# Attention products of 64 rows for two heads in place of 32 rows for four, with warming steps spread over the first batch, V on one queue and a new order of work

## The chip, the core and the metric

The kernel runs on one core of one Trainium2 chip. The metric is the device time of one execution in microseconds (us); lower is better. Five kinds of queues work side by side and each takes its instructions strictly in the order in which the kernel lists them: TensorE (PE, matrix products; its weight loads are shown apart as PEld), VectorE (DVE), ScalarE (ACT), GpSimd (POOL) and SyncE (SP, which only issues transfers). An instruction that waits holds up all that is listed behind it on its engine.

## The reference

For 8 batches, 8 heads, 576 positions and a head size of 64, the kernel computes causal attention in a window of 64 positions, puts the heads side by side (512 features), and feeds the result to a gated network with a spatial product. Cut to what matters:

```python
scores = scale * q @ k.T                        # per batch and head, 576 x 576
attn   = softmax(where(0 <= pos_q - pos_k < 64, scores, -1e9))
x      = (attn @ v), heads side by side          # 576 x 512 per batch
h      = relu(x @ w_in); u, v = h[..., :512], h[..., 512:]
v_n    = (v - mean(v)) / sqrt(var(v) + 1e-6)     # over the 512 features
v_s    = w_spatial @ v_n + b_spatial             # over the 576 positions
out    = (u * v_s) @ w_out
```

## The kernel before, in words

All work is cut into named steps. A step's name begins with its kind and holds its batch, and often its group `g` (heads 0 to 3, or 4 to 7), its pair of heads `u` within the group, or its block of 128 rows. Dependencies and buffers are declared with each step (`add(...)`), but the order on every engine, the engine itself and the buffer numbers come from one long hand-over string, `ORDER` (line 18 on): each word is `step:engine:buffers`. `DQ` is the transfer queue of SP. The costs that stand beside the steps (such as `("PE", 0.52)`) served whoever made the order; they do not act on the chip.

The steps, in the order in which one batch goes through them:

- `ldk`, `ldq` (line 382), `ldv` (line 404): loads of K, Q and V of a group. V comes in five pieces a group, `ldv{b}_{g}{c}`. For the very first group the five pieces are issued from ACT's queue (`dq = nc.scalar`), all others from SP's.
- `ck`, `cq`: casts of K and Q to 16 bits; `tk`, `tq`: their transposes on DVE (line 389). `cv`, `sl`, `su`, `s4`: the cast of V and the copies that make a second V, shifted by half a block. These casts and copies run on ACT (line 280), or on DVE or POOL (line 282), as the order says.
- `S` (line 457): scores of a group, in tiles of 32 rows by 64 columns, into a pair of PSUM tiles. `S{b}_r` (line 528) is the remainder, the last 64 positions of both groups.
- `E` (line 464): the exponential on ACT; `M` (line 467): the window mask, a minimum on DVE.
- `Z` (line 476): the sums of the softmax, products with a block of ones. Four heads are done side by side: each has 32 of the 128 output rows, and one PSUM bank holds all four. `Z{b}_r` (line 550) does it for the remainder.
- `N`, `n` (lines 508 and 510): the inverse of the sums, by a logarithm and an exponential on ACT, on 128 x 512 values for a group, 128 x 128 for the remainder.
- `P` (line 492): the products with V. A product gives 32 rows: every second feature of one head (`vhalf`), so that four heads lie side by side in a bank and the even and odd features in two banks (`f` = 0, 1). A group has 64 such products of 64 columns. `P{b}_r` (line 564) is the remainder.
- `X` (lines 501 and 572): the product with the inverse sums on DVE. Since features of a block are every second one of the heads, the rows of `w_in` are loaded with a step of two (line 308).
- `V{b}_j` (line 635), `V{b}_4` (lines 648 and 651), `U` (lines 690 and 695): products with `w_in`; `Vr` (line 615), `Ur` (line 703): evictions with relu on ACT; `Vb`, `Va` (lines 617 and 619): statistics on DVE; `L1`, `L2`: the inverse deviation on ACT; `A` (line 674): the normalization on DVE.
- `G` (lines 720 and 726): the spatial product; `Ge` (line 734): times u, on DVE; `O` (line 745): the product with `w_out`; `Oe` (line 598): eviction on ACT; `st`: store.

Besides there are the loads, casts and transposes of the weights (`ldwin`, `cwin`, `ldwsp`, `cwsp`, `W`, `We`, `ldwo`, `cwo`). `S` writes to two PSUM tiles of their own; `Z`, `P`, `V`, `U`, `G`, `O` and `W` share four banks, and a step on PE waits until its bank was read.

Ahead of all steps, 16 products of zeros (line 221) keep PE at work while the first loads are on their way.

Of the kernel before, what the change touches and what calls it, by code (L numbers as in the profile page):

```python
# [23 lines left out]
ldwin010:DQ:7 cv0_11:POOL ldwin011:DQ N0_0:ACT:0 s40_1:DVE S0_r:PE:0:1 sl0_11:DVE sl0_01:POOL ldk1_0:DQ:0
M0_10:DVE P0_0:PE:6:5 E0_r0:ACT:0 n0_0:ACT M0_11:DVE cwin100:POOL su0_10:POOL ldq1_0:DQ:1 E0_r1:ACT
su0_11:ACT M0_r:DVE ldk1_1:DQ:2 cwin101:ACT X0_00:DVE:0 Z0_r:PE:4 P0_r:PE:7 ldq1_1:DQ:3 N0_r:ACT:1
cwin111:POOL Z0_1:PE:6 X0_01:DVE n0_r:ACT ldwsp2:DQ:4 X0_r:DVE:0 N0_1:ACT:2 P0_1:PE:4:5 cwin110:DVE
n0_1:ACT ldwsp1:DQ:5 V0_4:PE:7 cwin001:ACT X0_10:DVE:1 X0_11:DVE cwin011:POOL cwin000:DVE V0_2:PE:6
Vr0_4:ACT:0 ldb:DQ:6 cwin010:ACT Vb0_4:DVE:0 ck1_0:POOL:0 ldwsp4:DQ:7 U0_4:PE:4 U0_3:PE:5 tk1_0:DVE:4
ldwsp0:DQ:0 Ur0_4:ACT:0 ldv1_00:DQ:2 cq1_0:POOL:1 Vr0_2:ACT:1 V0_1:PE:7 Va0_4:DVE Vb0_2:DVE:1 V0_0:PE:4  # L30
tq1_0:DVE:5 Vr0_1:ACT:2 ldwsp3:DQ:1 ck1_1:POOL:2 U0_0:PE:6 Vr0_0:ACT:3 Vb0_1:DVE:2 Ur0_3:ACT:1 S1_0:PE:0:1
tk1_1:DVE:0 ldwo10:DQ:2 cq1_1:POOL:3 V0_3:PE:7 E1_01:ACT:0 ldv1_01:DQ Va0_2:DVE cwsp2:POOL tq1_1:DVE:1
U0_1:PE:4 E1_00:ACT:1 ldv1_02:DQ cb:POOL Vb0_0:DVE:3 ldv1_03:DQ cwsp1:POOL Ur0_0:ACT:2 S1_1:PE:1:0
ldv1_04:DQ Vr0_3:ACT:4 M1_01:DVE ldq2_0:DQ:3 U0_2:PE:5 Ur0_1:ACT:3 M1_00:DVE cwsp4:POOL cwsp0:POOL
ldk2_0:DQ:4 E1_10:ACT:2 Vb0_3:DVE:4 ldv1_10:DQ:3 cwsp3:POOL Ur0_2:ACT:4 Va0_1:DVE Va0_3:DVE M1_10:DVE
W0:PE:6 E1_11:ACT:3 ldv1_11:DQ W2:PE:7 Va0_0:DVE W4:PE:4 ldv1_12:DQ We0:DVE cv1_00:POOL:2
W1:PE:5 L10:ACT:0 S1_r:PE:1:0 ldv1_13:DQ M1_11:DVE We1:ACT W3:PE:6 ldv1_14:DQ We2:DVE
cv1_01:POOL L20:ACT We4:ACT Z1_0:PE:5 sl1_00:DVE:2 Z1_1:PE:7 E1_r0:ACT:1 A0_2:DVE:0 N1_0:ACT:3
s41_0:DVE su1_00:POOL A0_1:DVE:1 n1_0:ACT A0_4:DVE sl1_01:POOL A0_0:DVE:2 su1_01:POOL N1_1:ACT:0
We3:DVE ldv2_10:DQ:0 P1_0:PE:4:5 E1_r1:ACT A0_3:DVE:3 cq2_0:ACT:0 M1_r:DVE ldq2_1:DQ:6 G0_0:PE:7  # L40
X1_00:DVE:2 ck2_0:POOL:1 ldv3_10:DQ:1 cwo10:ACT tq2_0:DVE:2 ldwo00:DQ:5 Z1_r:PE:6 n1_1:ACT G0_4:PE:4
ldk2_1:DQ:7 cv1_10:POOL:3 N1_r:ACT:1 ldwo11:DQ X1_01:DVE sl1_10:ACT:3 G0_3:PE:6 ldwo01:DQ Ge0_4:DVE:0
cv1_11:POOL tk2_0:DVE:3 ldq3_1:DQ:0 G0_2:PE:5 sl1_11:ACT su1_11:POOL ldv2_00:DQ:2 n1_r:ACT s41_1:POOL
su1_10:ACT Ge0_3:DVE:1 S2_0:PE:1:0 Ge0_2:DVE:2 P1_1:PE:4:6 ldk4_0:DQ:1 cq2_1:POOL:2 E2_00:ACT:0 Ge0_0:DVE:3
P1_r:PE:5 ldq3_0:DQ:3 X1_10:DVE:3 G0_1:PE:7 E2_01:ACT:1 ldk3_0:DQ:4 X1_11:DVE cwo00:ACT M2_01:DVE
V1_1:PE:4 Ge0_1:DVE:4 ldv2_01:DQ ck2_1:POOL:3 V1_0:PE:6 X1_r:DVE:1 tq2_1:DVE:0 ldv2_02:DQ V1_2:PE:7
Vr1_0:ACT:5 ldv3_00:DQ:3 Vr1_1:ACT:6 M2_00:DVE U1_2:PE:5 cwo11:ACT Vb1_1:DVE:5 Vr1_2:ACT:7 V1_3:PE:6
tk2_1:DVE:1 cwo01:ACT ldv2_03:DQ cq3_1:POOL:0 Z2_0:PE:4 Vr1_3:ACT:1 V1_4:PE:7 Vb1_0:DVE:0 N2_0:ACT:2
ldv2_11:DQ Vb1_2:DVE:1 Ur1_2:ACT:5 S2_1:PE:1:0 Oe0_4:ACT:0 Vb1_3:DVE:2 ck4_0:POOL:1 U1_3:PE:6 Vr1_4:ACT:2
Va1_1:DVE n2_0:ACT Vb1_4:DVE:4 U1_0:PE:4 E2_10:ACT:2 tk4_0:DVE:4 cq3_0:POOL:2 O0_2:PE:5 E2_11:ACT:3  # L50
Va1_2:DVE ldv2_12:DQ Va1_3:DVE O0_0:PE:7 Va1_0:DVE Va1_4:DVE M2_10:DVE Oe0_2:ACT:0 ldv2_13:DQ
M2_11:DVE ck3_0:POOL:3 U1_1:PE:5 Oe0_0:ACT:1 ldv2_04:DQ ldv2_14:DQ L11:ACT:1 O0_3:PE:7 L21:ACT
ldv3_01:DQ Ur1_1:ACT:0 A1_4:DVE Ur1_3:ACT:1 A1_3:DVE:4 ldv3_02:DQ S2_r:PE:1:0 A1_2:DVE:5 cv2_00:POOL:0
Z2_1:PE:5 E2_r0:ACT:0 ldv3_03:DQ tq3_1:DVE:5 U1_4:PE:6 Ur1_0:ACT:4 ldq4_0:DQ:6 N2_1:ACT:3 O0_1:PE:4
ldk3_1:DQ:7 A1_0:DVE:6 sl2_00:ACT:0 A1_1:DVE:7 cv2_10:POOL:1 tq3_0:DVE:0 G1_1:PE:5 Oe0_3:ACT su2_00:POOL
Oe0_1:ACT tk3_0:DVE:1 s42_0:ACT G1_0:PE:7 E2_r1:ACT ldv4_00:DQ:2 sl2_10:POOL:1 Ur1_4:ACT:2 Ge1_1:DVE:5
ldq4_1:DQ:2 P2_0:PE:4:6 s42_1:ACT su2_10:POOL ldk6_0:DQ:5 Ge1_0:DVE:6 n2_1:ACT S3_0:PE:1:0 ldv5_10:DQ:0
X2_00:DVE:0 cv3_00:POOL:2 P2_1:PE:5:7 ldq5_1:DQ:0 E3_00:ACT:0 ldv3_04:DQ X2_01:DVE G1_2:PE:4 st0_0:DQ
E3_01:ACT:1 X2_10:DVE:1 st0_1:DQ ck3_1:POOL:1 G1_3:PE:6 X2_11:DVE cq4_0:ACT:0 Ge1_2:DVE:7 V2_1:PE:5
Ge1_3:DVE:8 M2_r:DVE V2_2:PE:7 M3_00:DVE cq4_1:POOL:2 V2_3:PE:4 tk3_1:DVE:2 Vr2_2:ACT:0 Vr2_1:ACT:3  # L60
V2_0:PE:6 Vr2_3:ACT:4 M3_01:DVE S3_1:PE:1:0 tq4_1:DVE:3 Vr2_0:ACT:2 P2_r:PE:7 sl3_00:ACT:2 Z3_0:PE:5
Z2_r:PE:4 Vb2_2:DVE:3 O1_0:PE:6 N3_0:ACT:0 Vb2_3:DVE:5 N2_r:ACT:1 G1_4:PE:5 n2_r:ACT Vb2_0:DVE:1
n3_0:ACT O1_2:PE:4 E3_11:ACT:2 Va2_2:DVE Ge1_4:DVE:9 X2_r:DVE:0 O1_3:PE:5 Vb2_1:DVE:2 E3_10:ACT:3
M3_11:DVE O1_1:PE:7 Oe1_2:ACT:1 Va2_0:DVE Va2_1:DVE Va2_3:DVE Oe1_0:ACT:0 M3_10:DVE S3_r:PE:0:1
V2_4:PE:4 E3_r0:ACT:1 tq4_0:DVE:0 ck6_0:POOL:3 s43_0:POOL su3_00:POOL ldv4_10:DQ:3 ldv3_11:DQ cq5_1:POOL:1
st0_4:DQ ldv3_12:DQ ldv3_13:DQ ldk4_1:DQ:1 ldk5_1:DQ:3 ldv3_14:DQ Oe1_3:ACT U2_2:PE:6 E3_r1:ACT
Vr2_4:ACT:1 tq5_1:DVE:1 Oe1_4:ACT:0 S4_0:PE:0:1 cv3_10:POOL:3 Ur2_2:ACT:3 st1_4:DQ Vb2_4:DVE:0 P3_0:PE:5:4
Oe1_1:ACT ldq5_0:DQ:4 Z3_1:PE:6 Va2_4:DVE ldv4_11:DQ X3_00:DVE:2 U2_1:PE:7 L12:ACT:0 ldv4_12:DQ
L22:ACT N3_1:ACT:2 X3_01:DVE U2_0:PE:5 st1_0:DQ ck4_1:ACT:2 A2_2:DVE:0 ldv4_13:DQ A2_4:DVE
U2_3:PE:6 A2_3:DVE:1 Ur2_1:ACT:0 A2_1:DVE:2 E4_00:ACT:0 A2_0:DVE:3 U2_4:PE:4 M3_r:DVE G2_1:PE:7  # L70
# [743 lines left out]
```

## Time and profile before

| what | value |
|---|---|
| time, median of 3 runs | 208.84 us (207.15 to 210.27) |
| profiled execution: span from first to last instruction | 206.8 us (the page prints no other time of it) |
| busy: PE, DVE, ACT, POOL | 183.2, 165.0, 142.4, 88.5 us |
| mean granted clock of TensorE | 0.956 |
| first scores of batches 0, 1, 2, 3 | 9.67, 30.04, 45.75, 69.77 us |
| first scores of batches 4, 5, 6, 7 | 84.41, 109.78, 133.48, 154.74 us |
| last product of PE ends | 202.4 us |
| instructions | 7979 |

A profile holds one execution. Busy time of an engine is the time in which it had at least one instruction under way; the granted clock is the share of full speed that TensorE was allowed. A row of the groups gives the line, engine and operation, the tiles written and read with their shapes, then the busy time in us, the mean duration in ns, and the idle time of the engine just before such instructions with what ended it.

### The profile page before, as it was taken

To read this page: it belongs to the slowest core of one execution; us is meant where nothing else is said; L and a number is where in the kernel's file an instruction comes from. 1 tells how busy PE (TensorE), PEld (TensorE's weight loads), DVE (VectorE), ACT (ScalarE), POOL (GpSimd) and SP (SyncE) were. 2 spreads that over 40 slices of the span, in tenths; PEclk is the share of its full clock that TensorE was granted. 3 is DMA by queue.
4 is the path that set the end of the run, shared out by engine and by line. 5 is a ranking of instruction groups with operands and counts; after the bars stand their busy time and mean duration, and the time that the engine had idled before them with its cause. 6 is when DMAs were issued, how large, how long until landed. Compare 5 with 4: busy or idle time off the path is not lost.

```text
span 206.8 us, 7979 instructions
## 1 busy us (share of the span) xinstructions
PE 183.2 (89%) x3465; PEld 94.4 (46%) x3465; DVE 165.0 (80%) x297; ACT 142.4 (69%) x263; POOL 88.5 (43%) x101
## 2 busy tenths in 40 slices
PE   7326899599995999899997899999999999999991
...
DVE  4469899999889799999998689987878768646520
...
PEclk9955699999998899999999999999999999999998
...
GB/s 214 340 211 303 408 310 309 257 267 386 341 182 320 283 284 213 204 236 262 331 263 92 231 324 182 146 331 73 3 3 255 2 3 231 3 2 0 231 81 149
DMA packets 50197, 42.74 MB, mean 207 GB/s; under 512 B 39345, under 2 KB 39345, under 8 KB 50162
## 3 DMA queue, kind: packets, MB, share of 16 engines
...
q10 hardware_dynamic: 2384, 0.59, 1.3%
...
HBM read 32.79 MB, written 9.44 MB: 204 GB/s over the span
## 4 chain that ended last, share of the span: by engine, by line
PE 67%; DVE 17%; ACT 5%; DMA 4%; issue 3%; POOL 1%; SPq 0%; POOLq 0%; DVEq 0%
PE bank L720 16%; PE bank L745 12%; PE bank L635 11%; PE bank L690 10%; PE bank L492 4%; PE bank L648 4%; DVE e L467 4%; DMA nk<-in_k_dram 4%; DVE vn L674 3%; PE pair L457 3%; DVE qT L389 2%; PE bank L726 2%; PE bank L695 2%; DVE hs L282 2%; ACT vs L615 2%
## 5 line engine op out<-in xcount | busy, mean ns | idle before, releaser
L464 ACT ACTIVATE e<-pair 128x1024 f16<-128x1024 f32 x32 | 31.5, 1022 | 20.0 <-PE pair L457 12.5
L720 PE MATMUL bank<-wspT,vn 128*128 128x512 f16 (+1 forms) x160 | 39.8, 392 | 4.5 <-DVE vn L674 3.2
L615 ACT ACTIVATE vs<-bank 128x512 f16<-128x512 f32 (+1 forms) x40 | 23.1, 594 | 16.7 <-PE bank L635 12.9
L734 DVE TENSOR_TENSOR g<-bank,ru 128x512 f16<-128x512 f32 (+1 forms) x40 | 24.6, 629 | 11.8 <-PE bank L720 8.9
L690 PE MATMUL bank<-x,win 128*128 128x512 f16 x128 | 31.5, 379 | 0.1
L635 PE MATMUL bank<-win,x 128*128 128x512 f16 x128 | 30.9, 379 | 0.0
L745 PE MATMUL bank<-wout,g 128*128 128x512 f16 x128 | 30.7, 379 | 0.2 <-ACT ru L703 0.2
L617 DVE BATCH_NORM_STATS2 st<-vs 128x6 f32<-128x512 f16 (+1 forms) x40 | 26.2, 670 | 4.5 <-ACT vs L615 4.2
L703 ACT ACTIVATE ru<-bank 128x512 f32<-128x512 f32 (+1 forms) x40 | 21.8, 556 | 9.1 <-PE bank L695 5.5
L282 POOL CAST hk<-nk 128x1152 f16<-128x1152 f32 x14 | 16.9, 1204 | 25.0 <-DMA nk<-in_k_dram 22.1
L467 DVE TENSOR_TENSOR e<-e,mask 128x1024 f16<-128x1024 f16 x32 | 27.1, 867 | 0.3 <-ACT e L464 0.3
L282 POOL COPY hs<-hv 64x1024 f16<-64x1024 f16 (+3 forms) x29 | 26.1, 902 | 1.4
L282 POOL CAST hv<-nv 128x1024 f16<-128x1024 f32 (+1 forms) x18 | 18.0, 1008 | 19.1 <-DMA nv<-in_v_dram 19.0
L720 PEld LDWEIGHTS <-vn 128*128 128x128 f16 (+1 forms) x160 | 15.0, 100 | 23.4 <-DVE vn L674 4.4
L598 ACT COPY ob<-bank 128x512 f32<-128x512 f32 (+1 forms) x40 | 23.0, 586 | 3.4 <-PE bank L745 2.3
L501 DVE TENSOR_TENSOR x<-bank,lz 128x512 f16<-128x512 f32 x32 | 20.9, 678 | 3.7 <-ACT lz L510 2.4
L389 DVE STREAM_TRANSPOSE kT<-hk 128x576 f32<-128x576 f32 x16 | 19.7, 1239 | 3.7 <-ACT hk L280 2.9
L389 DVE STREAM_TRANSPOSE qT<-hq 128x576 f32<-128x576 f32 x16 | 19.7, 1239 | 1.8 <-POOL hq L282 1.6
L674 DVE TENSOR_SCALAR vn<-vs,mv,ln 128x512 f16<-128x512 f16 (+1 forms) x40 | 18.8, 524 | 2.7 <-ACT ln L664 2.6
L457 PE MATMUL pair<-qT,kT 32*64 32x128 f16 (+2 forms) x1024 | 12.9, 231 | 7.8 <-DVE qT L389 7.5
L745 PEld LDWEIGHTS <-g 128*128 128x128 f16 x128 | 12.1, 98 | 14.7 <-issue 1.0
L635 PEld LDWEIGHTS <-x 128*128 128x128 f16 x128 | 12.0, 98 | 14.5 <-issue 0.6
...
## 6 DMA issues: line engine op xcount, KB each, us to landing
...
```

The source lines that it names most:

```text
L282: ENG[e].tensor_copy(o, i)
L389: d = add(f"t{name}{b}_{g}", ("DVE", 1.09), key, lambda e: nc.vector.transpose(qt.t[:, :].rearrange("p (i j) -> p j i", j=18), h.t[:, :].b ...
L464: ex = add(f"E{b}_{g}{u}", ("ACT", 0.91), key, lambda e, u=u: nc.scalar.activation(e2[u].t[:, :, :], sc[u].t[:, :, :], AF.Exp, bias=0.0, s ...
L467: mins.append(add(f"M{b}_{g}{u}", ("DVE", 0.65), key, lambda e, u=u: nc.vector.tensor_tensor(e2[u].t[:, :, :], e2[u].t[:, :, :], mask[:, : ...
L615: rl = add(f"Vr{b}_{j}", ("ACT", 0.49), key, lambda e: nc.scalar.activation(vs.t[0:jn, :], m.t[0:jn, :], AF.Relu), deps=[pv], acq=[vs], us ...
L617: s1 = add(f"Vb{b}_{j}", ("DVE", 0.6), key + 0.02, lambda e: nc.vector.bn_stats(st6.t[0:jn, 0:6], vs.t[0:jn, :]), deps=[rl], acq=[st6], us ...
L635: nc.tensor.matmul(m.t[:, :], xr(b, r)[:, 128 * j:128 * j + 128], w_in_sb[r][:, 512:1024], start=(r == 0), stop=(r == 3))
L674: ENG[e].tensor_scalar(o[0:jn, :], VS[j].t[0:jn, :], mv_t[b % NSB][0:jn, j, 0:1], ln.t[0:jn, 5 + j:6 + j], ALU.subtract, ALU.mult)
L690: nc.tensor.matmul(m.t[:, :], w_in_sb[r][:, 128 * i:128 * i + 128], xr(b, r), start=(r == 0), stop=(r == 3))
L720: nc.tensor.matmul(m.t[:, :], w[0:kn, 128 * i:128 * i + 128], wspT[kk][0:kn, 0:512], start=(kk == 0), stop=(kk == 4))
L734: lambda e, m=m, g=g, ru=ru, n=n: nc.vector.tensor_tensor(g.t[:, 0:n], m.t[:, 0:n], ru.t[:, 0:n], ALU.mult),
L745: nc.tensor.matmul(m.t[:, :], G[r][0].t[:, 128 * j:128 * j + 128], w_out_sb[r][:, :], start=(r == 0), stop=(r == 3))
```

## The change

In `Z`, `P` and `X` a step now serves a pair of heads, not four. Each product with V gives all 64 features of one head, so that two heads fill the 128 rows of a bank; a group has two steps of `Z` (`Z{b}_{g}{u}`) and two of `P`, each with a bank of its own, where it had one of each with one and two banks. `N` and `n` run once for every pair, so twice a group, on 128 x 512 values; for the remainder on 128 x 256 values. `X` multiplies each pair's products with the pair's own inverse. There are six `lz` buffers for four. The features of a block are now contiguous, and so are the rows of `w_in` that are loaded.

The 16 products of zeros ahead of the steps become 25 steps `D0` to `D24` of two products each, which the order places among PE's work up to the middle of batch 0. The first group's V is issued from SP's queue like the others. The order is written anew as a whole, on all engines: steps stand elsewhere, many casts and copies change their engine, and buffers have other numbers. Counted over the whole order:

| steps | before | after |
|---|---|---|
| `Z` and `P` of groups, on PE | 16 and 16 | 32 and 32 |
| `N` and `n` of groups, on ACT | 16 and 16 | 32 and 32 |
| casts and copies of K, Q, V, weights on POOL | 90 | 64 |
| the same on ACT (`ck`, `cq`, `cv`, `sl`, `su`, `s4`) | 2, 4, 2, 5, 2, 6 | 6, 4, 2, 9, 3, 10 |
| the same on DVE (`ck`, `cq`, `cv`, `sl`, `su`, `s4`) | 0, 0, 0, 2, 2, 2 | 1, 1, 5, 4, 7, 1 |

The diff, cut to its core:

```diff
 ORDER = """
-ldk0_0:DQ:0 ldq0_0:DQ:1 ldk0_1:DQ:2 ldq0_1:DQ:3 ldv0_00:DQ:0 ldv0_01:DQ ldv0_02:DQ ldv0_03:DQ ldv0_04:DQ
-ck0_0:ACT:0 tk0_0:DVE:0 ldv0_10:DQ:1 cq0_0:ACT:1 tq0_0:DVE:1 ldv0_11:DQ ck0_1:POOL:2 S0_0:PE:0:1 tk0_1:DVE:2
-ldv0_12:DQ cq0_1:POOL:3 E0_00:ACT:0 ldv0_13:DQ E0_01:ACT:1 ldv0_14:DQ tq0_1:DVE:3 cv0_00:POOL:0 ldwin100:DQ:4
-sl0_00:POOL:0 M0_00:DVE ldwin101:DQ cv0_01:ACT S0_1:PE:0:1 ldwin110:DQ:5 M0_01:DVE s40_0:POOL ldwin111:DQ
...
+ldq0_0:DQ:0 ldk0_0:DQ:1 D14:PE:0 ldk0_1:DQ:2 ldq0_1:DQ:3 D12:PE:1 ldv0_00:DQ:0 ldq1_0:DQ:4 D23:PE:2
+ldk1_0:DQ:5 ldv0_10:DQ:1 D15:PE:3 cq0_0:POOL:0 ldv0_11:DQ D22:PE:0 D6:PE:1 tq0_0:DVE:0 D0:PE:2
+ck0_0:ACT:1 ldv0_01:DQ D16:PE:3 tk0_0:DVE:1 ck0_1:ACT:2 ldv0_02:DQ S0_0:PE:0:1 tk0_1:DVE:2 D21:PE:0
+E0_00:ACT:0 ldv0_12:DQ D7:PE:1 D11:PE:2 cq0_1:DVE:3 E0_01:ACT:1 ldv0_03:DQ D24:PE:3 tq0_1:DVE:3
+M0_01:DVE cq1_0:ACT:0 ldwin100:DQ:6 S0_1:PE:0:1 M0_00:DVE D5:PE:0 E0_10:ACT:2 tq1_0:DVE:4 D17:PE:1
+D2:PE:2 ldv0_04:DQ E0_11:ACT:3 D4:PE:3 ck1_0:DVE:1 ldv0_13:DQ D1:PE:0 S0_r:PE:0:1 M0_10:DVE
+ldv0_14:DQ Z0_00:PE:1 E0_r0:ACT:0 cv0_10:DVE:0 Z0_10:PE:2 E0_r1:ACT M0_11:DVE ldwin110:DQ:7
+Z0_01:PE:3 N0_10:ACT:0 D10:PE:0 sl0_10:DVE:0 cv0_00:DVE:1 N0_01:ACT:1 ldb:DQ:0 M0_r:DVE N0_00:ACT:2
+sl0_00:DVE:1 Z0_r:PE:2 su0_00:DVE ldwin111:DQ Z0_11:PE:0 N0_r:ACT:3 D9:PE:3 n0_00:ACT cv0_01:DVE
+ldwin101:DQ D8:PE:1 su0_01:DVE sl0_01:POOL n0_10:ACT su0_10:DVE D13:PE:2 ldwin000:DQ:1 n0_01:ACT
...
-    for i in range(16):
-        nc.tensor.matmul(bank(4 + i % 2), scratch[:, 0:128], scratch[:, :], start=True, stop=True)
-    ones = cpool.tile([128, 32], f16, name="ones")
+    ones = cpool.tile([128, 64], f16, name="ones")
...
-                                 st.t[:, 512 * f:512 * f + 512], moe_w_in[256 * g + f:256 * g + 256:2, cs]),
+                                 st.t[:, 512 * f:512 * f + 512], moe_w_in[256 * g + 128 * f:256 * g + 128 * f + 128, cs]),
...
-        dq = nc.scalar if (b, g) == (0, 0) else nc.sync
...
-        zb = buf("bank", f"z{b}_{g}")
-                for hh in range(4):
-                    nc.tensor.matmul(zb.t[32 * hh:32 * hh + 32, :], ones[:, :],
-                                     e2[hh // 2].t[:, hh % 2, :], start=True, stop=True)
...
-        ob = [buf("bank", f"o{b}_{g}{f}") for f in (0, 1)]
-                        for hh in range(4):
-                            nc.tensor.matmul(ob[f].t[32 * hh:32 * hh + 32, 64 * c:64 * c + 64],
-                                             vhalf(vv, c // 2, hh, f),
-                                             e2[hh // 2].t[:, hh % 2, 64 * c:64 * c + 64],
+        for u in (0, 1):
+            zb, ob = buf("bank", f"z{b}_{g}{u}"), buf("bank", f"o{b}_{g}{u}")
+            lz = buf("lz", f"lz{b}_{g}{u}")
+                    for w in (0, 1):
+                        nc.tensor.matmul(zb.t[64 * w:64 * w + 64, :], ones[:, :], e2[u].t[:, w, :],
+                                         start=True, stop=True)
...
+                    for c in range(8):
+                        vv = hv.t if c % 2 == 1 or c == 0 else hs.t
+                        for w in (0, 1):
+                            nc.tensor.matmul(ob.t[64 * w:64 * w + 64, 64 * c:64 * c + 64],
+                                             vv[:, c // 2, 2 * u + w, :],
+                                             e2[u].t[:, w, 64 * c:64 * c + 64],
+                                             start=True, stop=True)
...
-        lzd = inverse_steps(f"{b}_r", zb, lz, z, key + 0.03, 128)
+        lzd = inverse_steps(f"{b}_r", zb, lz, z, key + 0.03, 256)
...
+    for i in range(NWARM):
+        m = buf("bank", f"warm{i}")
+        def emit_D(e, m=m):
+            for _ in range(2):
+                nc.tensor.matmul(m.t[:, :], scratch[:, 0:128], scratch[:, :], start=True, stop=True)
+        add(f"D{i}", ("PE", 0.43), -2.0, emit_D, acq=[m], mode="f")
```

More of the change, by code (lines that the diff above doesn't have):

```diff
@@ L24 @@
[L24 to L70, printed above, removed]
-tk4_1:DVE:2 ck5_1:POOL:0 sl3_10:POOL:3 Ur2_4:ACT:4 su3_10:POOL n3_1:ACT E4_01:ACT:1 G2_2:PE:4 Ge2_1:DVE:0
```

254 lines of the change are left out of this document (152 added, 102 removed).

## The prediction

> **What bounds the kernel now.** I read the page's first two parts (busy time; 40 slices of 5.17 us), then busy time by stage, then groups by form, VectorE's groups early and late, the chain of waits, and single stretches of TensorE.
>
> ```profile
> PE 183.2 (89%) x3465; PEld 94.4 (46%) x3465; DVE 165.0 (80%) x297; ACT 142.4 (69%) x263; POOL 88.5 (43%) x101
> PE   7326899599995999899997899999999999999991
> DVE  4469899999889799999998689987878768646520
> PEclk9955699999998899999999999999999999999998
> ```
>
> The averages hide two stages: DVE is the fuller engine in slices 3 to 14, PE from slice 15 on, and the clock is near half in slices 3 to 5. By stage (stretch, its length, then busy us of PE, weight loads, DVE, ACT, POOL; clock; DMA), cut where M0_00, S1_0, S2_0, S3_0, S5_0 and S7_0 start:
>
> ```profile
> 14.34:30.00 15.66, 12.90 (x292) 7.02 (x292) 14.64 (x24) 10.45 (x20) 11.66 (x13) 0.67 0.97 336
> 30.00:45.70 15.70, 13.19 (x309) 7.48 (x308) 15.70 (x29) 13.62 (x26) 13.32 (x18) 1.00 1.01 273
> 45.70:69.80 24.10, 21.53 (x407) 10.25 (x407) 21.77 (x34) 17.46 (x33) 14.65 (x14) 0.93 0.97 312
> 109.80:154.70 44.90, 42.91 (x984) 23.16 (x984) 37.65 (x70) 32.91 (x62) 20.81 (x22) 1.00 0.59 159
> 154.70:202.40 47.70, 47.70 (x624) 23.72 (x620) 28.80 (x60) 28.61 (x56) 0.00 (x0) 1.00 0.27 92
> ```
>
> DVE sets the end of the front (up to S3_0 at 69.8), PE the rest up to 202.4; 4.4 us of last eviction and store follow. ACT has 12 us free in 109.8:154.7.
>
> Groups that the change touches (count, busy us, mean ns, idle before):
>
> ```profile
> L476 PE MATMUL bank<-e,ones 128*32 128x512 f16 x64 | 7.4, 412 | 0.1
> L508 ACT ACTIVATE lz<-bank 128x512 f32<-128x512 f32 x16 | 9.5, 596 | 1.3 <-PE bank L476 1.3
> L510 ACT ACTIVATE lz<-lz 128x512 f32<-128x512 f32 x16 | 10.1, 629 | 0.3
> ```
>
> DVE's step A first in 9.67:69.8, then in 150:200; the same instruction costs twice as much while POOL is busy:
>
> ```profile
> L674 DVE TENSOR_SCALAR vn<-vs,mv,ln 128x512 f16<-128x512 f16 x8 | 7.0, 893 | 0.0
> L674 DVE TENSOR_SCALAR vn<-vs,mv,ln 128x512 f16<-128x512 f16 x12 | 4.3, 401 | 1.0 <-ACT ln L664 1.0
> ```
>
> TensorE in order of time (start, length): a score step, then the first rounds of V_4, two 64-column tiles each:
>
> ```profile
> 145.16 0.77 PE L457 MATMUL pair<-qT,kT 32*64 32x128 f16 x64
> 145.88 0.40 PE L648 MATMUL bank<-win,x 128*64 128x512 f16 x1
> 145.89 0.40 PE L651 MATMUL bank<-wout,g 128*64 128x512 f16 x1
> 146.12 0.38 PE L648 MATMUL bank<-win,x 128*64 128x512 f16 x1
> ```
>
> **The sum's base.** The page prints a span of 206.8 and no time of its own. The runs are 207.15 to 210.27, so 0.35 to 3.5 us lie around the span; I take 2.0, which puts the profiled execution on the median, 208.84.
>
> **TensorE.** A Z step runs four 32-row strips at once, 0.22 us in the chain of waits. After, each pair has a Z of its own, two 64-row strips over the same 512 columns, 0.22 each: 16 more steps, +3.5. Z_r goes from one round of 128 columns to two, 0.06 to 0.11, eight times: +0.4. P is 64 products in 0.54 to 0.64, middle 0.57, or 34 ns for four at once. After, a pair's P is 16 products in eight rounds of two. No row has 128x64 products of 64 columns. V_4 is nearest, the same tile shape: its rounds start every 0.22, four full products of 512 columns take 0.86, so 4 to 7 ns lie on top of the columns. 64 columns are 27 ns, a round 33, a step 0.27; 32 steps make 8.6 against 16 x 0.57 = 9.1: -0.5. Lower end 27 ns, 1.7 less. Upper end by the score step: rounds of eight tiles, the longest columns 192, 128, 128, 128, twice, in 0.69: 86 ns a round, 60 of them columns; 25 on top give 52 ns, 0.42 a step, 4.8 more. So +3.4 over eight batches.
> What counts lies behind S3_0. Listed there are ten more Z (+2.2), six Z_r (+0.3), 23 P at 0.27 for 11 at 0.57 (-0.1) and one O (0.87) that the new order puts later: **+3.4** with rounding, a list of 129.6 for 126.2 (measured 132.6). A change of tile shape leaves about 0.09 us (the last full product's columns end near 132.42, Z starts at 132.51); there are 57 of them behind S3_0 before, 59 after: **+0.2**.
>
> On weights the row comes first: four 32-column loads and 64 columns take 34 ns together. The Trainium skill's "TensorE: Matmul & The Clock Gate", section "LDWEIGHTS (loading the stationary operand)", prices a load by its columns divided by 1.2, in ns: 27 for 32 columns and 53 for 64. Unhidden, its estimate would be 54 ns a round before, which the trace denies, and 80 after, some 12 us more for P.
>
> **ScalarE.** Two Ln and two Exp of 512 columns per group in place of one each: 9.5 + 10.1 = 19.6 busy; those of the remainder go from 128 to 256 columns, 274 and 311 ns to about 381 (the exp of 256): +1.4. The order also moves casts and copies off POOL (90 steps to 64): ACT gets four K casts, four s4, four sl and one su more, at 1.05, 0.33, 0.75 and 0.95, about 9. At back-to-back prices (Ln 0.50, Exp 0.53, evictions 0.51) ACT's list grows from 134.9 to 163.0. Between S5_0 and S7_0 it is 31.6 beside PE's 41.7 before, and 44.3 beside 44.2 after. ACT ran 4% over its list there (32.9): 46.1; PE with 21 shape changes: 46.1 too. So the slack that hid Ln and Exp is gone: evictions queue behind casts on ACT, and PE waits for banks, of which a group now takes four, not three. Lower end 0. Upper end by 45.7:69.8, where DVE's list was 18.8, PE's 18.6: 2.3 of DVE idle, 12%, so 5.6. Nearest is S4_0 to S5_0, PE 23.6 plus 0.8 of changes beside DVE 21.7, in 25.4: 4%, **+1.9**, which I take.
>
> **Loads.** V of the first half-group leaves ACT's queue (five issues from 0.85 to 5.66; ck0_0 starts at 5.70, right behind) for SP, at 1.19 an issue (five in 5.96). With Q and K of batch 1 also ahead, SP gets to the last V-half load of w_in about 6 us later, near 20.7; 4.9 to landing and a 0.65 cast put the first V step at 26.3 for 23.2 now. DVE has 3.5 us of transposes, M and X to do meanwhile: 0; if that cover is gone, 3. In exchange the first Q and K share no engine with V's 0.58 MB, 2.1 us at the 276 GB/s of the first 10 us; I take 1.3: tk0_1 at 9.1 instead of 10.42. Contiguous w_in rows carry the same bytes, X_r the same elements: 0.
>
> **The front.** At back-to-back prices (transpose 1.1; M, X, Vb, Ge 0.6; A 0.32; copies of V 0.2 to 0.35) DVE's list from tk0_1 to S3_0 is 46.7 before, 49.8 after (17 copies of V instead of 6). It took 59.3: 7.7 of stretching (A 8 x 0.49, M 12 x 0.17, copies 3 x 0.5, rest 0.2) and 4.9 idle. POOL's list there falls from 35.4 to 23.8, which leaves 5.2 of the stretching; the 11 more copies are of the form that stretched (819 ns for 258) and put back about 2.5. Warming steps fill the PE gap from 5 to 9.7 us behind which the clock fell; warm, Z, P and V0_4 on the chain (0.62, 0.85, 1.68 from 21.75) save 1.3, of which DVE idled 1.0. Their 10.8 us (25 x 0.43) lie beside DVE work: 0, up to 4 if cold or behind a full bank. S3_0 then comes at 9.1 + 49.8 + 7.7 + 4.9 - 1.0 = 70.5: **+0.8**. Lower end, no stretching and no idle: 58.9, -10.9. Upper end, start as now and V uncovered: 75, +5.
>
> The stretching row bears on a page: the Trainium skill's "SBUF — State Buffer", section "Who interferes with whom", says that DVE's 2-port copies and tensor_scalar, and its operations on two SBUF inputs, block against GpSimd. The trace agrees (893 ns for 401). By that alone, with fewer POOL steps, the sum would be 2.5 lower.
>
> Sum: 206.8 + 0.8 + 3.4 + 0.2 + 1.9 = 213.1 of span, with 2.0 around it **215.1**; this case alone holds 213 to 218.
>
> **Rivals.** *DVE's front runs at its pitch*, unstretched and without idle: S3_0 at 58.9, 215.1 - 11.7 = 203.4. It gains over 2% once S3_0 comes before 60.2. For it: POOL gives up a third of its list. Against: 11 more copies on DVE, and loads that come no faster. *ACT keeps slack*: its waits 0 and stretching 5.2: 215.1 - 1.9 - 2.5 = 210.7. For it: 69% busy; against: the equal lists. *ACT becomes the bound*: 5.6 for 1.9, 218.8. *Weights show* as in the score step: five eighths of 4.8, 218.1. *The warming does not hold the clock* or stands in the way: up to 4, 219, only where DVE idles for it.
>
> **Numbers.** Forecast 0.38; ACT slack 0.25; DVE at pitch 0.19, of it 0.16 under the line; ACT bound 0.10; weights 0.05; warming 0.03. About 2% is what a measurement of this kernel can tell from no change, so the lines are 204.7 and 213.0: faster 0.16, same 0.25 + 0.03 = 0.28, slower 0.56. Range 204 to 221: it leaves out part of DVE at pitch, and upper ends that fall together, under 0.2.
>
> **What would show it.** S3_0 near 70; PEclk full in slices 3 to 5; Z twice as often at 0.22, P steps of 0.27; ACT some 170 busy, with PE waiting for its evictions between S5_0 and S7_0; A still near 0.89 early. S3_0 before 61, or ACT with idle time late, would make me wrong.

## The result

The changed kernel takes 204.75 us (median of 20 runs, 203.04 to 208.94), the kernel before 209.32 beside it (20 runs, 205.22 to 212.72). The ratio is 0.987, with a 95% interval of 0.983 to 0.991: a gain of 1.3%, inside the 2% that the prediction called no change. It had put the most chance on slower, at 215.1, and its range, 204 to 221, just holds the time. The profiled execution has a span of 203.7 us for 206.8. Executions come in a fast and a slow state, and ratios compare fast ones alone, whereas the medians (whose quotient is 0.978) are over all; the profiles of `b_sh240` and `a_sh96` are of slow ones, so that their spans and starts are not compared.

The page of the changed kernel, busy time and slices of 5.09 us:

```profile
PE 189.8 (93%) x2923; PEld 97.7 (48%) x2923; DVE 164.0 (80%) x310; ACT 167.6 (82%) x308; POOL 63.2 (31%) x75
PE   7678999798969999999999999999999999999992
DVE  4699989999999889889789898879957795647420
PEclk9999999999999999999999999999999999999999
```

The clock is full from the start, ACT has 25 us more to do, and from slice 13 to the last but one PE is busy for nine tenths or more. By stage (as before: length, then busy us of PE, weight loads, DVE, ACT, POOL; clock; DMA), cut at the starts of S2_0, S3_0, S5_0 and S7_0:

```profile
47.58:66.11 18.53, 16.95 (x275) 8.32 (x270) 18.14 (x31) 15.93 (x31) 11.61 (x11) 1.00 0.87 252
66.11:104.11 38.00, 38.00 (x706) 20.57 (x704) 33.60 (x63) 35.06 (x65) 15.95 (x17) 1.00 0.83 238
104.11:149.71 45.60, 45.56 (x717) 23.66 (x711) 40.26 (x76) 44.29 (x86) 17.19 (x17) 1.00 0.82 228
149.71:199.30 49.59, 49.50 (x593) 25.49 (x591) 30.18 (x61) 36.58 (x69) 0.00 (x0) 1.00 0.23 83
```

ACT is busy for 44.29 of 45.60 us between S5_0 and S7_0, as forecast, yet PE has 0.04 us idle there. S3_0 starts at 66.11 (before 69.77, forecast 70.5). From there to PE's end, first before, then after:

```profile
69.80:202.46 132.66, 129.80 (x2390) 67.06 (x2386) 105.58 (x196) 94.29 (x179) 43.12 (x44) 1.00 0.54 162
```

```profile
66.11:199.72 133.61, 133.47 (x2008) 69.72 (x2006) 104.04 (x198) 115.98 (x217) 33.14 (x33) 1.00 0.61 177
```

PE's busy time grew by 3.67 us, but the stretch by only 0.95: before, PE was idle for 2.86 us of it, after for 0.14. The whole account of the span: front -3.66, PE's work +3.67, PE's idle time -2.72, the last eviction and store -0.4 (4.4 to 4.0); together -3.1.

For most of the time in which PE stood idle before, the chain of waits names no releaser. Two such places, of 0.82 and 0.83 us:

```profile
85.18 0.40 PE bank L492 x37
85.57 0.82 issue
86.39 0.39 PE bank L492 x27
...
117.38 0.37 PE bank L492 x34
117.75 0.83 issue
118.58 0.41 PE bank L492 x30
```

A step P breaks off in the middle of its 64 products and goes on 0.8 us later, though none of them waits for anything.

### The profile page after: what moved, and what is told of

The parts are those of the page before. It is cut to its first block, busy times and chain, and to the rows that moved or that the text cites. A ratio compares the mean times of both kernels' runs of the same rounds, so it can differ in the third digit from the quotient of the medians.

```text
span 203.7 us, 6932 instructions
## 1 busy us (share of the span) xinstructions
PE 189.8 (93%) x2923; PEld 97.7 (48%) x2923; DVE 164.0 (80%) x310; ACT 167.6 (82%) x308; POOL 63.2 (31%) x75
## 3 DMA queue, kind: packets, MB, share of 16 engines
q1 hardware_dynamic: 50162, 42.23, 69.4%
## 4 chain that ended last, share of the span: by engine, by line
PE 68%; DVE 15%; DMA 8%; ACT 5%; issue 1%; SPq 1%
PE bank L722 15%; PE bank L747 12%; PE bank L637 10%; PE bank L692 10%; DMA wi<-in_moe_w_in_dram 5%; PE pair L464 4%; PE bank L498 4%; DMA nk<-in_k_dram 3%; PE bank L487 3%; DVE e L474 3%; PE bank L650 3%; PE bank L728 2%; DVE st L619 2%; PE bank L697 2%; DVE kT L402 2%; DVE qT L402 2%
## 5 line engine op out<-in xcount | busy, mean ns | idle before, releaser
L722 PE MATMUL bank<-wspT,vn 128*128 128x512 f16 (+1 forms) x160 | 37.5, 379 | 0.0
L747 PE MATMUL bank<-wout,g 128*128 128x512 f16 x128 | 31.3, 379 | 0.0
L619 DVE BATCH_NORM_STATS2 st<-vs 128x6 f32<-128x512 f16 (+1 forms) x40 | 26.3, 673 | 3.4 <-ACT vs L617 3.2
L600 ACT COPY ob<-bank 128x512 f32<-128x512 f32 (+1 forms) x40 | 23.2, 587 | 3.7 <-PE bank L747 3.1
L474 DVE TENSOR_TENSOR e<-e,mask 128x1024 f16<-128x1024 f16 x32 | 24.9, 794 | 1.0 <-ACT e L471 1.0
L295 POOL COPY hs<-hv 64x1024 f16<-64x1024 f16 (+2 forms) x17 | 16.5, 975 | 13.6 <-DVE hv L295 13.0
L513 ACT ACTIVATE lz<-bank 128x512 f32<-128x512 f32 x32 | 18.6, 602 | 2.0 <-PE bank L487 1.9
L515 ACT ACTIVATE lz<-lz 128x512 f32<-128x512 f32 x32 | 19.6, 631 | 0.1
L692 PEld LDWEIGHTS <-win 128*128 128x128 f16 x128 | 11.7, 97 | 15.1 <-issue 1.3
L295 POOL CAST hq<-nq 128x1152 f16<-128x1152 f32 x11 | 12.8, 1172 | 19.2 <-DMA nq<-in_q_dram 17.1
L747 PEld LDWEIGHTS <-g 128*128 128x128 f16 x128 | 11.7, 98 | 13.4 <-issue 0.5
```

Of the source, the lines that this page charges most:

```text
L295: ENG[e].tensor_copy(o, i)
L474: mins.append(add(f"M{b}_{g}{u}", ("DVE", 0.65), key, lambda e, u=u: nc.vector.tensor_tensor(e2[u].t[:, :, :], e2[u].t[:, :, :], mask[:, : ...
L600: cpy = add(f"Oe{b}_{j}", ("ACT", 0.49), key, lambda e: nc.scalar.copy(view(), m.t[rows, :]), deps=[po, first], acq=[] if half else [ob], ...
L619: s1 = add(f"Vb{b}_{j}", ("DVE", 0.6), key + 0.02, lambda e: nc.vector.bn_stats(st6.t[0:jn, 0:6], vs.t[0:jn, :]), deps=[rl], acq=[st6], us ...
L692: nc.tensor.matmul(m.t[:, :], w_in_sb[r][:, 128 * i:128 * i + 128], xr(b, r), start=(r == 0), stop=(r == 3))
L722: nc.tensor.matmul(m.t[:, :], w[0:kn, 128 * i:128 * i + 128], wspT[kk][0:kn, 0:512], start=(kk == 0), stop=(kk == 4))
```

## Experiments

Kernels whose name begins with b are the kernel before with an edit, those with a the changed kernel. The ratio is to the kernel before. S3_0 and the gaps are of one execution each. The last column is explained under "TensorE's own instructions".

| kernel | ratio, 95% interval | S3_0 us | border gaps us |
|---|---|---|---|
| before | 1 | 69.8 | 3.8 |
| after | 0.987 (0.983 to 0.991) | 66.1 | 0 |
| `b_64` | 1.040 (1.033 to 1.048) | 71.3 | 0 |
| `a_32` | 1.067 (1.047 to 1.087) | 65.7 | 3.8 |
| `b_warm` | 1.039 (1.024 to 1.054) | 72.6 | 10.7 |
| `b_warm2` | 1.055 (1.047 to 1.063) | 74.3 | 11.7 |
| `a_cold` | 0.996 (0.988 to 1.003) | 66.0 | 1.0 |
| `a_vact` | 0.997 (0.992 to 1.003) | 68.4 | 0.1 |
| `a_s1late` | 1.029 (1.022 to 1.036) | 73.0 | 0 |
| `a_steps` | 0.998 (0.993 to 1.004) | 69.6 | 0.3 |
| `a_pool` | 0.983 (0.977 to 0.990) | 64.6 | 0.9 |
| `a_late` | 0.989 (0.982 to 0.996) | 66.5 | 0.1 |
| `a_more` | 1.022 (1.014 to 1.029) | 65.2 | 0 |
| `b_sh96` | 1.096 (1.086 to 1.105) | 75.1 | 17.1 |
| `b_sh240` | 1.005 (0.996 to 1.014) | | 5.7 |
| `b_sh32` | 0.998 (0.990 to 1.007) | 69.4 | 3.2 |
| `a_sh96` | 1.001 (0.992 to 1.010) | | 1.9 |
| `a_pool32` | 0.996 (0.991 to 1.002) | 67.0 | 1.3 |

### The products and the order, each without the other

`b_64` takes the new Z, P, X, N and n and the contiguous w_in rows into the old order, each pair's steps where the group's step stood:

```diff
-Z3_0:PE:5 ... N3_0:ACT:0 ... n3_0:ACT ... P3_0:PE:5:4
+Z3_00:PE:5 Z3_01:PE:4 ... N3_00:ACT:0 ... N3_01:ACT:5 ... n3_00:ACT n3_01:ACT ... P3_00:PE:5 P3_01:PE:4
```

> The kernel before with the products alone changed: Z, P, N and n of a group are cut into two pairs of heads that stand next to each other where the one step stood, 64 rows each, banks and inverse buffers given anew, no other step moved. Theory 'the new order pays, the products cost': PE's list grows by 3.4 us (16 Z more at 0.22, Z_r 0.4, P slightly less) and ACT's by 18, so 3 to 6 us slower than before, 212 to 215. Theory 'half the products do away with TensorE's own gaps': the gaps of about 0.8 us inside P with the releaser 'issue' (at 85.6 and 117.8 in the profile before, 1.0 at 20.1) go, 2.7 us, and P's rounds start every 31.5 ns, so PE's loss is repaid: 207.5 to 210.5, same as before. The trace tells: count PE's idle with releaser issue behind the first scores of batch 3 (before 1.6 us).

`a_32` does the reverse: the old steps in the new order, at the place of the later pair, for which 15 steps of PE and DVE moved.

> The changed kernel (new order, warming steps, V on SP) with the old products of 32 rows for four heads: each pair of Z, P, N and n steps is one step at the place of the later one; X steps that would stand ahead of their P go behind it. Theory 'the new order pays, the products cost': 3.4 us less on PE's list and 18 on ACT's, 2 to 5 us faster than the changed kernel, 200 to 203. Theory 'half the products do away with gaps': TensorE's own gaps inside P come back (about 0.8 each), and with the later places of P the time is that of the changed kernel or up to 4 us more, 204 to 209.

Neither part pays by itself: +4.0% and +6.7%. `b_64` is nearest to what the forecast described, new steps with the old order's waits: 4.0% more, where the forecast had 3.0% (215.1/208.84). From its S3_0 to PE's end:

```profile
71.27:211.00 139.73, 134.54 (x1992) 69.53 (x1986) 108.45 (x197) 104.09 (x199) 43.16 (x44) 1.00 0.53 161
```

So S3_0 comes 1.5 us later than before, PE is busy for 4.7 us more behind it, and idle for 5.2 us in place of 2.9. It waits for a normalization on DVE and, in small pieces, for ACT:

```profile
PE bank L713 <- DVE vn L667: 2.0, 2, 1.1
PE bank L738 <- ACT lz L504: 0.7, 2, 0.4
PE bank L489 <- ACT ru L696: 0.5, 1, 0.5
```

`a_32` keeps the early S3_0 (65.7), so the front's gain is the order's and not the products'. Its loss comes later: of 149.0 us from S3_0 to PE's end PE is idle for 12.8, among them two waits for DVE's g and one for x, 3.2 and 1.9 us, in an order that was made for pairs. How much of the 6.7% is the misfit, and how much the products, it can't tell.

### The warming steps

`b_warm` adds 14 warming products to the old order behind the first scores. Its steps write to banks still in use, so that part of the sums and products is lost. `b_warm2` gives them free banks.

```diff
-S0_0:PE:0:1
+S0_0:PE:0:1 D0:PE:4 D1:PE:5 D2:PE:6 D3:PE:7
```

> The kernel before with 14 warming steps more (two products of zeros each), between its score, sum and V products of batch 0, and nothing else changed. Theory 'the cold clock cost the front': granted clock 1.0 from 10 to 25 us in place of about 0.6, Z, P and V0 of batch 0 at full speed, first scores of batch 3 at 68.5 or earlier instead of 69.8, and 1 to 2.5 us faster than before. Theory 'VectorE sets the front': clock full as well, but the first scores of batch 3 stay within 0.7 us of 69.8, and the time within 0.7 us of before.

> The kernel before, with 14 full-width warming products (0.43 us each at full clock) behind the first scores, each in a bank that is free there; order, products and queues otherwise as before. Theory (a full clock in slices 3 to 5 is worth what DVE idles for PE there, about 1 us): granted clock above 0.9 between S0_0 and S1_0 (0.67 before), S3_0 at 68.5 to 69.3 for 69.77, time 0.2 to 0.7% less than before. Rival (warming gives the new kernel its whole gain in the front): S3_0 at 66 to 67, time 1.2 to 1.6% less. Third (the steps stand in front of Z and P on PE): S3_0 at 71 or later, time 0.5% more or worse.

`b_warm2` is 5.5% slower, with a better clock (0.974 in the mean for 0.956). The first two theories fall. The third has its two numbers met, but not by its mechanism, the work of the added steps: PE stands still for 2.3, 2.9 and 3.2 us at 24.2, 52.1 and 78.2 us, the last two far behind the warming steps, and waits for nothing that the profile names.

`a_cold` takes the 17 warming steps behind the first scores out of the new order.

> The changed kernel without the 17 warming steps behind the first scores; the eight ahead of them stay (16 products, as many as before). Theory 'the cold clock cost the front': the clock falls to half from about 13 us on, sums and V of batch 0 and the first V products run at half speed, first scores of batch 3 at 67.5 to 69 instead of 66.1, 1 to 3 us slower than the changed kernel, 206 to 208. Theory 'VectorE sets the front': within 0.7 us of the changed kernel, 204 to 205.5.

The clock falls again (0.955 in the mean for 0.999), S3_0 stays (66.0), the span is 0.8 us longer, and two gaps of together 1.0 us, of the kind seen in `b_warm2`, are new in it. So the warming steps did hold the clock, but a gain from the clock itself isn't shown; the 0.9% in the ratio may be the gaps.

### The front

`a_vact` issues the first V from ACT's queue again:

```diff
+        dq = nc.scalar if (b, g) == (0, 0) else nc.sync
-                           lambda e, c=c, sn=sn: nc.sync.dma_start(
+                           lambda e, c=c, sn=sn: dq.dma_start(
```

> The new kernel, with V of the first half-group issued from ACT's queue again, right behind the first four loads of Q and K; everything else as in the new order. Theory (the front's early start, tk0_1 at 9.15 for 10.42, comes from keeping these 0.58 MB out of the way of the first Q and K): tk0_1 back near 10.4, ck0_0 later by what five issues take on ACT, S0_0 near 9.7, and S3_0 1.0 to 1.5 us later, near 67.3; time 0.5 to 0.7% above the new kernel's, a ratio of about 0.985 to the kernel before. Rival (DVE waits later for loads in any case, so an early start is only waited away): tk0_1 at 10.4, S3_0 within 0.4 us of 66.1, the same time.

tk0_1 went from 9.15 to 10.45, as both said. S3_0 came 2.3 us later and the time rose by 1.1% (0.9974/0.9869): the early start is carried through to the end, and the rival falls. The later start is 1.3 of the 2.3 us; the other 1.1 are idle time of DVE between tk0_1 and S3_0 (3.1 us for 2.0), whose cause these runs don't settle.

`a_s1late` puts loads, casts, transposes and scores of batch 1's first group back behind batch 0; `a_steps` leaves the loads, casts and transposes early and moves only the scores and what follows from them.

```diff
-... S1_0:PE:0:1 sl0_11:DVE ... E1_00:ACT:1 ... Vr0_3:ACT:3 ...
+... sl0_11:DVE ... Vr0_3:ACT:3 S1_0:PE:0:1 E1_00:ACT:1 E1_01:ACT:0 M1_00:DVE M1_01:DVE Z1_00:PE:1 ...
```

> The new kernel, with the loads, casts and transposes of Q and K of batch 1's first group, and the scores, exp, mask, sums and reciprocal that follow from them, put back behind the work of batch 0, where the old order had them; V still on SP, everything else as in the new order. Theory (DVE's idle time of the front fell from 4.9 to about 2.3 us because batch 1's first scores stand ready as a second supply of DVE steps): DVE idle before S3_0 back to 4 to 5 us, S3_0 at 68 to 69, time 1.0 to 1.4% above the new kernel's. Rival (the idle time was of the missing w_in and Q loads, and the order of the steps does not matter): S3_0 within 0.5 us of 66.1, or earlier, because V and w_in now pass through SP sooner; time the same or 0.3% less.

> The new kernel, with the loads, casts and transposes of Q and K of batch 1's first group early as there, and only the scores, exp, mask, sums and reciprocal that follow from them put back behind the work of batch 0. Theory (their early place gives DVE and ACT steps to do while w_in and V are awaited): S1_0 near 33 for 20.6, DVE idle before S3_0 1 to 3 us more, S3_0 at 67.5 to 69, time 0.6 to 1.4% above the new kernel's. Rival (only the early loads and casts matter, whose delay cost a wait of 6.6 us when they were put back too): S3_0 within 0.5 us of 66.1, time within 0.3% of the new kernel's.

The first lost 4.3% against the changed kernel, three times what was expected, since DVE has K's cast at its head and waits for the late load:

```profile
DVE hk L280 <- DMA nk<-in_k_dram: 6.6, 1, 6.6
```

The second has no such wait and still loses 1.2%, with S3_0 at 69.6: DVE is idle for 5.6 of the 57.5 us from 8.5 to 66, against 2.7. So the early place of batch 1's first scores is worth 3.5 us in the front, and 2.9 of that is idle time of DVE. Its two longest waits in `a_steps` are 1.8 us for an eviction and 1.7 for the inverse deviation; that the early masks fill just these is likely, but not shown.

`a_pool` gives 13 copies and casts of V of batches 0 and 1 to POOL.

```diff
-cv0_10:DVE sl0_10:DVE cv0_00:DVE sl0_00:DVE cv0_01:DVE su0_10:DVE cv0_11:DVE cv1_00:DVE ...
+cv0_10:POOL sl0_10:POOL cv0_00:POOL sl0_00:POOL cv0_01:POOL su0_10:POOL cv0_11:POOL cv1_00:POOL ...
```

> The new kernel, with 13 copies and casts of V of batches 0 and 1 on POOL in place of DVE (about 4.5 us of DVE's list in the front, some 9 us on POOL). Theory of the prediction on record (what counts in the front is DVE's list and its stretching, 7.7 us there by POOL's 23.8 us of steps and DVE's own copies): DVE's list falls by 4.5, stretching of A, M and transposes rises by 2 to 3, S3_0 1 to 2.5 us earlier, time 0.5 to 1.2% less than the new kernel's. Rival (POOL's copies take twice as long and the products with V wait for them): PE waits for hs and hv of POOL in batches 0 and 1, S3_0 at 67 or later, time 0.5% more or worse.

S3_0 at 64.6, 1.5 earlier; 0.35% less time than the changed kernel, where 0.5 to 1.2 were expected, and their intervals overlap: faster isn't shown. Of the 4.5 us taken off DVE's list, 1 went back in stretching (masks 995 ns for 940, A 546 for 512) and 2 in idle time, part of it at copies that now wait for POOL's cast.

### ScalarE

`a_late` takes 18 late casts and copies off ACT, `a_more` puts five on it:

```diff
-s45_0:ACT sl6_10:ACT s45_1:ACT sl6_00:ACT s46_0:ACT s46_1:ACT ck7_0:ACT cv7_00:ACT cq7_0:ACT ...
+s45_0:POOL sl6_10:POOL s45_1:POOL sl6_00:POOL s46_0:POOL s46_1:POOL ck7_0:POOL cv7_00:POOL cq7_0:POOL ...
```

```diff
-cq6_0:POOL su5_10:POOL su6_10:POOL su6_00:POOL ck6_1:POOL
+cq6_0:ACT su5_10:ACT su6_10:ACT su6_00:ACT ck6_1:ACT
```

> The new kernel, with 18 casts and copies of batches 5 to 7 (13 us of ACT's time between about 100 and 160 us) on POOL in place of ACT. Theory (ACT at 97% between S5_0 and S7_0 holds nobody up, because the new order puts every eviction ahead of the step that needs its bank): ACT falls to about 85% there, PE idle stays at 0 to 0.3 us, stretch S5_0 to S7_0 within 0.4 us of 45.6, total time within 0.4%. Rival of the prediction on record (ACT's crowding costs 1.9 us there, hidden in what PE's busy time shows): S5_0 to S7_0 at 43.7 to 44.2, total 0.7 to 0.9% less. Third (POOL's work stretches DVE, which then holds PE up): DVE's busy time 2 to 4 us more, PE waits for DVE's g or x, total 0.5 to 1.5% more.

> The new kernel with five casts and copies of batches 5 and 6 (4.6 us at ACT's prices) on ACT in place of POOL, between S5_0 and S7_0, where ACT is busy 44.3 of 45.6 us. Theory (ACT's slack there is only what is left of the stretch, 1.3 us; past that it sets the pace): S5_0 to S7_0 at 48 to 49.5, PE waits of 2.5 to 4 us for ACT's evictions, time 1.2 to 2% above the new kernel's. Rival (ACT's steps wait in banks and buffers that the order has spare, and the end of the kernel, where ACT has 13 us free, takes them up): under 1 us more there, time within 0.4%.

S5_0 to S7_0 in the one and in the other (same columns as above):

```profile
105.00:150.70 45.70, 45.59 (x715) 23.79 (x711) 41.79 (x75) 38.45 (x75) 26.86 (x30) 1.00 0.80 223
```

```profile
105.10:156.30 51.20, 46.23 (x719) 23.95 (x713) 40.88 (x77) 49.89 (x91) 12.90 (x12) 1.00 0.73 203
```

With 5.8 us less on ACT the stretch stays (45.7 for 45.6): ACT held nobody up. With 5.6 more busy time it grows by exactly as much, 5.6, and the time by 3.5%: ACT is the bound then. I had expected 2.4 to 3.9 more, from back-to-back prices. PE's longest waits in it (the DVE step of the first waited 2.7 us for ACT's `lz`):

```profile
PE bank L622 <- DVE x L491: 2.1, 1, 2.1
PE bank L732 <- ACT ru L690: 0.9, 1, 0.9
PE bank L622 <- ACT vs L602: 0.8, 1, 0.8
PE bank L483 <- ACT ob L585: 0.7, 1, 0.7
```

### TensorE's own instructions

The pages list a queue of transfers that no line issues (packets, MB, share of the DMA engines). Before and after:

```profile
q8 instruction: 27, 0.44, 0.9%
```

```profile
q8 instruction: 23, 0.38, 0.8%
```

The trace has each packet: 16384 bytes. There are 27 packets for 6930 of PE's records (a weight load and a product count as two), 23 for 5846: by this, a packet is 256 instructions of 64 bytes each.

I numbered PE's records from zero, with the seven or eight that its sequencer runs, and looked at the gaps that nothing explains. In the kernel before they lie at 449, 3009, 4033 and 4289, in `b_warm2` at 705, 1729, 2497, 3521, 4545, 5057 and 6337: all are 193 plus a multiple of 256. I call these places borders.

Packet i, counted from zero, starts at the earliest when PE is 28 instructions short of number 193 + 256 i (up to 40 in other runs). In the kernel before and the changed one it starts within 1.6 us of that point behind 160 us, where there is little DMA work, and mostly 1 to 5 us behind it until then. What it brings begins with number 449 + 256 i: each gap ends 2.2 to 2.9 us (once 3.3) behind its packet's start. So 256 instructions have to last for the packet's delay and some 2.4 us more. A step P of 32-row products is 128 instructions in 0.57 us, one of 64-row products 32 in 0.25.

The column "border gaps" adds up the gaps that end so. The profile gives some of them in part to another wait: of the 1.16 us at 4033 in the kernel before, the chain gives 0.76 to DVE, and two of the four in `a_32` (1.71 and 0.86 us) are put down to DVE as a whole. The Trainium skill's "Runtime: NRT & Kernel Launch", section "Instruction fetch mechanics", says that an engine's instructions are refilled in 16 KiB blocks of 256 while the current one runs, at a cost that is mostly hidden. The blocks agree; the cost is hidden here only where 256 instructions last long enough.

The test is to move the borders and nothing else: the warming products at the very start, cut into narrower pieces, give the same columns in more instructions.

```diff
     for i in range(16):
-        nc.tensor.matmul(bank(4 + i % 2), scratch[:, 0:128], scratch[:, :], start=True, stop=True)
+        for c in range(0, 512, 128):
+            nc.tensor.matmul(bank(4 + i % 2)[:, c:c + 128], scratch[:, 0:128], scratch[:, c:c + 128], start=True, stop=True)
```

`b_sh96` is this; `b_sh240` cuts to 57 and 64 columns, `b_sh32` to 256. `a_sh96` cuts the first eight warming steps of the changed kernel to 128, and `a_pool32` those of `a_pool` to 256.

> The kernel before, with its 16 warming products of 512 columns at the very start cut into 64 of 128 columns: the same columns, 96 more TensorE instructions (a weight load and a product each) ahead of the first scores, all later work as it was. In the trace TensorE's instructions come in by packets of 16 KB (27 for 6930 instructions), and all of the short gaps that the page calls issue lie at instruction 193 + a multiple of 256, ending 2.3 to 2.6 us behind the start of a packet's record. Theory (a gap is a late packet: 256 instructions that run in under about 4 us outrun it): the gaps move to the work that stands 96 instructions earlier in the list, again at 193 + a multiple of 256; by the spacing of the old trace five of them would be over 2 us each, most behind S2_0, so 3 to 9 us more, 1.5 to 4.5%. Rival (the gaps belong to the 32-row products with V, wherever they stand in the list): gaps as before in the same P steps, near 85.6 and 117.8, time within 0.4%.

> The same with the warming products cut into 136 pieces of 57 or 64 columns: 240 more TensorE instructions ahead of the first scores. Theory (late packets): the borders of the packets move 16 instructions later than in the kernel before (256 - 240); gaps still at 193 + a multiple of 256; by the old spacing they sum to 1.8 us in place of 3.5, so the time is 0 to 1% less, and clearly less than with 96. Rival (more instructions, more time): 240 cost more than 96. Rival (gaps belong to the 32-row products): the same time as with 96, within 0.4%.

> The kernel before, with its 16 warming products cut into 32 of 256 columns: 32 more TensorE instructions ahead of the first scores. By the spacing of the old trace this is the best shift of all, with gaps of 1.5 to 2.5 us less in sum, mostly that at 449 of the front. Theory (the kernel before already stands near the best place for its borders): time 0 to 0.8% less than the kernel before's, still over the new kernel's. Rival (the new kernel's whole gain is the luck of its borders): 1.3% less or more, as fast as the new kernel.

> The new kernel, with the 16 warming products ahead of the first scores cut into 64 of 128 columns: 96 more TensorE instructions, the same columns. Theory (fewer instructions for P make the packets last longer, so the border's place matters little): gaps at packet borders sum to 0.5 to 3 us, time 0.2 to 1.2% above the new kernel's, against 9.6% for the same shift in the kernel before. Rival (the new order is only lucky in where its borders fall): 5 us of gaps or more, time 3% or more above.

> The new kernel with 13 copies and casts of V on POOL in place of DVE (as run before: 0.35% less than the new kernel, gaps of 0.73 and 0.12 us at borders) and 32 more TensorE instructions ahead of the first scores. Theory: gaps under 0.3 us in sum; span 202.0 to 202.6, ratio to the kernel before 0.979 to 0.984. Rival (gaps in the front are waited away behind DVE, and a longer start costs): span as without the 32, 202.6, or more.

48 more short products at the start cost 9.6%. The chain of waits of `b_sh96`:

```profile
75.87 0.55 PE bank L493 x53
76.42 5.04 issue
81.46 0.32 PE bank L493 x9
...
146.40 0.56 PE bank L493 x56
146.97 4.81 issue
151.78 0.30 PE bank L493 x6
```

Seven gaps, 17.1 us in all, each at 193 plus a multiple of 256 and in other places of the work than before. That the gaps belong to certain steps P is refuted, and so is "more instructions, more time": with 240 the time is back within 0.5% of the kernel before. The sums were worse than expected (13.3 more for 3 to 9, 5.7 for 1.8, 3.2 for at most 2); I had taken one delay for all packets, and the traces show delays from nothing to 5 us. None of the three shifts tried gives the kernel before a better place, `b_sh32` neither, so nothing here says that the gain is the luck of its borders; other shifts were not run. The same shift of 96 costs the changed kernel 1.4%, a little over the 0.2 to 1.2 expected, with a single gap of 1.92. In the orders and product forms taken apart, the gaps follow the form: 3.8 and 3.8 us with 32 rows (before, `a_32`), 0 and 0 with 64 (`b_64`, after). Over all runs they are 3.2 to 17.1 us in the seven kernels with 32 rows and 0 to 1.9 in the eleven with 64. `a_pool32` missed: gaps of 1.3 us in place of under 0.3, and S3_0 2.4 later than in `a_pool`, with DVE waiting 2.5 us for an eviction where it waited 1.1; why the front moved is open.

## Why the prediction was wrong

- **PE's work: right.** +3.6 forecast (Z, Z_r, P, O, shapes), +3.67 in busy time. P's rounds came every 31.7 ns in the median step (31.0 to 35.1 behind S3_0), for the 33 taken; the weights do not show. The clock held, too.
- **PE's idle time: not seen.** The sum carried the old stretch's gaps along, 2.86 us behind S3_0, as if they belonged to the work. Of these, 2.05 us by the chain of waits, and at most 2.81, are borders of instruction packets. The 64-row products take away what causes them: P issues half as many instructions. I had the "issue" lines in the chain and gave them no cause. This is -2.7.
- **The front: the step that failed most.** S3_0 = 9.1 + 49.8 + 7.7 + 4.9 - 1.0 = 70.5 against 66.11. Start (9.15) and list hold: DVE is busy for 54.9 us in between, 49.8 and 5.2 of stretching (A 8 x 0.11, M 12 x 0.27, copies 9 x 0.12), where 7.7 were taken. A, the copies, and the masks before and after:

```profile
L676 DVE TENSOR_SCALAR vn<-vs,mv,ln 128x512 f16<-128x512 f16 x8 | 3.7, 512 | 0.0
L295 DVE COPY hs<-hv 64x512 f16<-64x512 f16 x9 | 3.3, 375 | 0.2
L467 DVE TENSOR_TENSOR e<-e,mask 128x1024 f16<-128x1024 f16 x12 | 9.8, 841 | 0.0
L474 DVE TENSOR_TENSOR e<-e,mask 128x1024 f16<-128x1024 f16 x12 | 11.2, 940 | 0.0
```

  A did not stay near 893 ns, and the copies cost 375, not 819 (the 2.5 that they were to put back came from no row); the masks rose. The sum is lower by the 2.5 that stood under the rule of the Trainium skill's "SBUF — State Buffer", section "Who interferes with whom". That it fits to a tenth is partly luck, since the forecast scaled all stretching with the length of POOL's list, and this does not follow it: with POOL busy for 41.8, 35.1 and 26.6 us from 8.5 to 66 (before, `a_pool`, after), A takes 893, 546 and 512 ns. What the rows show instead is that only instructions with a step of POOL beside them are slow. Before, that holds for all eight A (394 to 1227 ns). After, seven of the eight have at most 0.07 us of POOL beside them and take 387 to 413 ns; the eighth has two of its casts:

```profile
39.19 1.30 DVE L676 TENSOR_SCALAR vn<-vs,mv,ln 128x512 f16<-128x512 f16 x1
39.20 1.15 POOL L295 CAST hk<-nk 128x1152 f16<-128x1152 f32 x1 [1.59 <-DMA nk<-in_k_dram]
40.29 0.67 POOL L295 CAST hv<-nv 128x512 f16<-128x512 f32 x1
```

  Of the twelve masks, the five without POOL beside them take 664 to 680 ns, and five of the other seven 997 to 1644 (the remaining two 650 and 675). In `a_pool`, four A beside POOL take 635 to 750, the other four 391 to 401. So the new order set A free, and put masks beside POOL's casts and copies. Idle time was 2.0 (66.11 - 9.15 - 54.9), where 3.9 were carried over from an order that no longer existed. `a_steps` shows what shortens it: batch 1's scores, placed early.
- **The cover for V's later loads held**: V0 starts at 24.4 (before 23.2, forecast 26.3), and DVE's waits behind it are short, the longest in sum 1.0 us for evictions.
- **ACT's crowding: mechanism not there.** Busy 167.6 in all (forecast 170), 44.3 between S5_0 and S7_0 (forecast 44.3 at pitch, 46.1 stretched), and PE waits for nothing. The 4% over the list, taken from S4_0 to S5_0 of the old order, did not come. `a_more` shows how close it was: 1.3 us of room. The likeliest rival named on record, ACT keeps slack, had this and the sum of the stretching right, and stops at 210.7 for want of PE's gaps and DVE's idle time.

With the failed terms replaced, 215.1 - 4.4 (front) - 1.9 (ACT) - 2.7 (PE's gaps) - 0.4 (tail) gives 205.7: the profiled span of 203.7 with the same 2.0 around it. The errors of the front and of ACT had one direction because both came from taking the old order's waits as a property of the work. PE's gaps are another matter: they belong to the form of the products, and `b_64` has none in the old order. That it ended near the forecast is therefore partly luck: PE's work grew by 4.7 us there and its other waits by more than the gaps saved.

Two smaller slips of the prediction changed nothing: the terms of the +3.4 behind S3_0 add up to 3.3, and in slices 11, 12 and 14 PE, not DVE, is the fuller engine (from 45.7 to 69.8 us the two are about even, 21.5 and 21.8).
